# Attention pairs with q and k in 1.5 KB runs, evacuations ordered ahead of masks, and full-row stores

## The chip, the cores and the metric

The kernel runs on one core of a Trainium2 chip. The time is device microseconds (us) from launch to the end of the program on that core. Before the change the median of three runs is 192.61 us, with 190.53 and 195.77 as lowest and highest. The profile is of one further execution, whose span is 193.9 us.

A core has five engines that run their own instruction lists in order: TensorE (PE, with its weight loads as PEld), VectorE (DVE), ScalarE (ACT), GpSimd (POOL) and SyncE (SP). Sixteen DMA engines move data between HBM and the on-chip SBUF. TensorE writes to PSUM, from which VectorE and ScalarE read. Between engines there are semaphores, which the tile framework places from the order of the statements; within an engine the order of the statements is the order of execution.

## The reference

Two steps. First attention over 4 batches of 8 heads, 768 tokens, head size 64. "Retrieval" heads see all earlier tokens; the other heads see only the first 4 tokens and the last 64. Then a soft mixture of experts over the 3072 tokens of width 512, with 8 experts of 4 slots.

```python
scores = scale * q @ k.T                      # per head, 768 x 768
mask = causal if head is retrieval else causal & (first 4 columns | last 64 tokens)
a = exp(scores where mask); a = a / a.sum(-1)
x = (a @ v) with heads side by side           # (4*768, 512)

logits = x @ phi                              # (3072, 32)
d = exp(logits); d /= d.sum(over tokens)      # dispatch
slot_input = d.T @ x                          # (32, 512)
slot_out[e] = relu(slot_input[e] @ w1[e]) @ w2[e]     # 8 experts, 4 slots each
c = exp(logits); c /= c.sum(over slots)       # combine
out = c @ slot_out                            # (3072, 512) float32
```

## The kernel before

The 32 heads are worked through as 16 pairs (n = 0 to 15), four pairs to a batch. A pair's exponentials come in six chunks (c = 0 to 5), each of up to 1024 elements per partition for the two heads. Weights, q, k and v are loaded as float32 and cast to bf16 by GpSimd's DMAs. The parts that matter:

```python
raw  = tile_pool("raw", bufs=3);  qkT = tile_pool("qkT", bufs=2);  vfp, ptp, xp: bufs=2
scp = PSUM pool, bufs=2 (scores, logits, expert and output sums)
trp = PSUM pool, bufs=2 (everything transposed);  pvp = PSUM pool, bufs=2

def load_qk(n, which):                        # 8 tokens = 2 KB to a partition, 96 partitions
    t = raw.tile([96, 2, 512], BF16)
    nc.gpsimd.dma_start(t, src[b, h:h + 2].rearrange("h (p s) d -> p h (s d)", s=8))

def transposes(n, which):
    tp = trp.tile([P, 8, 96], BF16, tag="tr")
    ... 16 TensorE transposes of 96x64
    if which == "q":   # the queries end up in a permuted token order
        nc.vector.tensor_copy(dst.rearrange("c (i s p) -> c i s p", s=8, p=16),
                              tp.rearrange("c s (i p) -> c i s p", p=16))
    else:
        nc.vector.tensor_copy(dst.rearrange("c (p s) -> c p s", s=8), tp.rearrange("c s p -> c p s"))

def vfar(n):                                  # v times the head's far mask
    for i in range(2):
        nc.gpsimd.tensor_mul(t[:, i], vbs[n % 5][:, i, :4, :], fmask[...].to_broadcast([P, 4, 65]))

def scores(n, c):
    ... matmuls into sc
    nc.scalar.activation(pT[n][:, :, o:o + ln], sc[:, :, :ln], ACT.Exp, scale=scale)
    if c in (0, 1, 2): nc.vector.tensor_mul(x, x, m)      # near mask, at once

def pvmm(n, i): ...                           # rows i of a @ v, 65 columns (the last is the sum)
def norm(n, half): ...                        # reciprocal and multiply on VectorE, into xb
def x_transpose(n): ...                       # 6 transposes, one copy to xT on VectorE

def logits_exp(b):
    nc.scalar.activation(expC[b], lgs[b][:ES], ACT.Exp)                       # 32 x 768
    for c in range(2):                        # the same again, put back into token order
        nc.scalar.activation(expT[:, b, 384*c:384*(c+1)].rearrange("c (i p s) -> c i s p", s=8, p=16),
                             lgs[b][:, c, :384].rearrange("c (i s p) -> c i s p", s=8, p=16),
                             ACT.Exp, accum_out=colpart[...])

# set-up on VectorE: masks, then a column of ones in all five v buffers
transposes(0, "k"); transposes(0, "q"); head_mask(0); head_mask(1)
for t in vbs: V.memset(t[:, :, :, D:], 1.0)

for n in range(NP + 1):
    load_qk(n + 3, "k"); load_qk(n + 3, "q"); load_v(n + 3); w_load(1 or 2); vfar(n)
    for c in range(6):
        scores(n, c)
        # last = n - 1, the pair before
        c == 0: pvmm(last, 0..2); norm(last, 0)
        c == 1: transposes(n + 1, "q")
        c == 2: pvmm(last, 3); x_transpose(n - 2)
        c == 3: transposes(n + 1, "k");  if n % 4 == 1: logits_mm(b, all); logits_exp(b)
        c == 4: pvmm(last, 4);           if n % 4 == 2: dispatch(b)
        c == 5: pvmm(last, 5); norm(last, 1)
        # n % 4 == 2, c == 0: exp_tokens(b)
    n < 3: two more head_masks on VectorE

... last w2 loads, in halves of 256 columns
x_transpose(15); logits_mm(3, (3,)); logits_exp(3); exp_tokens(3); dispatch(3)   # whole batch at a time
... slot sums, 64 expert matmuls "hp", relu, 16 transposes, 24 small row sums "rp"

# second expert matmul and outputs, one half of 256 columns after the other
for e4, gs in ((0, (0, 1, 2, 3)), (1, (0, 1))):
    for x in range(2): second(x, e4, gs)
for x in range(2):
    for g in (2, 3): second(x, 1, (g,))
    V.tensor_copy(slot_out[:, cs], sp[x])
    for t in range(6):
        op = scp.tile([P, 4, 256], F32)       # 4 matmuls of 256 columns
        V.tensor_mul(ots[t][:, 0:2, cs], op[:, 0:2], rrow...)
        for r in (2, 3): nc.scalar.activation(ots[t][:, r, cs], op[:, r], ACT.Copy, scale=rrow...)
        nc.sync.dma_start(ov[:, 4*t:4*t+4, cs], ots[t][:, :, cs])    # runs of 1 KB
```

Of the kernel before, what the change touches and what calls it, by code (L numbers as in the profile page):

```python
# [38 lines left out]
def kernel(  # L39
# [41 lines left out]
    phif = single([P, 4, ES], F32, "phif")  # L81
# [10 lines left out]
    fmask = single([P, H, 4], BF16, "fmask")  # L92
# [5 lines left out]
    r1 = single([P, H], F32, "r1")  # L98
    thr = single([P, H], F32, "thr")
    vbs = [single([P, 2, 6, 65], BF16, f"vb{i}") for i in range(5)]  # L100
# [3 lines left out]
    def load_qk(n, which):  # L104
        b, h = n // 4, 2 * (n % 4)
        src, d = (q, qraw) if which == "q" else (k, kraw)
        t = raw.tile([96, 2, 512], BF16, tag="r" + which, name="r" + which)
        nc.gpsimd.dma_start(t, src[b, h:h + 2].rearrange("h (p s) d -> p h (s d)", s=8))  # L108
        d[n] = t
# [25 lines left out]
    def transposes(n, which):  # L135
        src = (qraw if which == "q" else kraw)[n]
        tp = trp.tile([P, 8, 96], BF16, tag="tr", name="tp" + which)
        for s in range(8):
            for hh in range(2):
                nc.tensor.transpose(tp[64 * hh:64 * hh + 64, s, :], src[:, hh, 64 * s:64 * s + 64],  # L140
                                    ident[:96, :96])
        dst = qkT.tile([P, S], BF16, tag="T" + which, name="T" + which)
        if which == "q":
            nc.vector.tensor_copy(dst.rearrange("c (i s p) -> c i s p", s=8, p=16),  # L144
                                  tp.rearrange("c s (i p) -> c i s p", p=16))
            qT[n] = dst
        else:
            nc.vector.tensor_copy(dst.rearrange("c (p s) -> c p s", s=8), tp.rearrange("c s p -> c p s"))  # L148
            kT[n] = dst

    def vfar(n):
        h = 2 * (n % 4)
        t = vfp.tile([P, 2, 4, 65], BF16, tag="vf", name="vf")
        for i in range(2):
            nc.gpsimd.tensor_mul(  # L155
                t[:, i], vbs[n % 5][:, i, :4, :],
                fmask[:, h + i, :].rearrange("p (j o) -> p j o", o=1).to_broadcast([P, 4, 65]))
        vf[n] = t

    def scores(n, c):  # L160
# [11 lines left out]
        nc.scalar.activation(pT[n][:, :, o:o + ln], sc[:, :, :ln], ACT.Exp, scale=scale)  # L172
        h = 2 * (n % 4)
        if c == 0:
            x, m = pT[n][:, :, 0:512], msk[:, h:h + 2, 0:512]
        elif c == 1:
            x = pT[n][:, :, 512:1024].rearrange("p h (a c) -> p h a c", a=2)
            m0 = msk[:, h:h + 2, 256:512]
            m = bass.AP(tensor=m0.tensor, offset=m0.offset, ap=[m0.ap[0], m0.ap[1], [0, 2], [1, 256]])
        elif c == 2:  # L180
            x, m = pT[n][:, :, 1024:1408], msk[:, h:h + 2, 256:640]
        else:
            return
        nc.vector.tensor_mul(x, x, m)  # L184

    def pvmm(n, i):
        if i % 3 == 0:
            pv[n] = pvp.tile([P, 3, 2, 65], F32, tag="pv", name="pv")
        for hh in range(2):
            for j in range(i + 1):  # L190
                vv = vbs[n % 5] if i - j <= 1 else vf[n]
                o = BLK[j, i]
                nc.tensor.matmul(pv[n][:, i % 3, hh, :], pT[n][:, hh, o:o + 128], vv[:, hh, j, :],  # L193
# [12 lines left out]
    def x_transpose(n):  # L206
        b, hp = n // 4, n % 4
        tp = trp.tile([P, S], BF16, tag="tr", name="tpx")
        for i in range(6):
            nc.tensor.transpose(tp[:, i * 128:(i + 1) * 128], xb[b][:, i, hp * 128:(hp + 1) * 128], ident)  # L210
        nc.vector.tensor_copy(xT[:, hp], tp)
# [3 lines left out]
    def logits_mm(b, dbs):  # L215
        if dbs[0] == 0:
            lgs[b] = scp.tile([P, 2, 512], F32, tag="sc", name="lg")
        for db in dbs:
            for c in range(2):
                nc.tensor.matmul(lgs[b][:, c, :384], phi4[:, db].rearrange("p g s -> p (g s)"), xT[:, db, 384 * c:384 * (c + 1)],  # L220
                                 start=(db == 0), stop=(db == 3))

    def logits_exp(b):
        expC[b] = small.tile([ES, S], BF16, tag="expC", name="expC")
        nc.scalar.activation(expC[b].rearrange("c (a t) -> c a t", a=2), lgs[b][:ES, :, :384], ACT.Exp)
        for c in range(2):
            nc.scalar.activation(  # L227
                expT[:, b, 384 * c:384 * (c + 1)].rearrange("c (i p s) -> c i s p", s=8, p=16),
                lgs[b][:, c, :384].rearrange("c (i s p) -> c i s p", s=8, p=16),
                ACT.Exp, accum_out=colpart[:, 2 * b + c:2 * b + c + 1])  # L230

    elgs = {}
    expC = {}

    def exp_tokens(b):
        tp = trp.tile([P, 6, ES], BF16, tag="tr", name="tpe")
        for i in range(6):
            nc.tensor.transpose(tp[:, i, :], expC[b][:, i * 128:(i + 1) * 128], ident[:ES, :ES])
        elgs[b] = small.tile([P, 6, ES], BF16, tag="elg", name="elg")
        nc.vector.tensor_copy(elgs[b], tp)  # L240

    def dispatch(b):
        sp = trp.tile([P, DM], F32, tag="tr", name="slp")
        for i in range(6):
            g = i % 4
            nc.tensor.matmul(sp[32 * g:32 * g + 32, :], elgs[b][:, i, :], xb[b][:, i, :],
                             start=(i < 4), stop=(i + 4 >= 6))
        if b == 0:
# [5 lines left out]
        else:  # L254
            nc.vector.tensor_copy(slot_bf[:, 1], sp)
# [6 lines left out]
    nc.sync.dma_start(phif, moe_phi.rearrange("(do di) s -> di do s", di=P))  # L262
    diff = single([P, P], F32, "diff")
    dist = single([P, 256], F32, "dist")
    nc.gpsimd.iota(diff, pattern=[[1, P]], base=0, channel_multiplier=-1,
                   allow_small_or_imprecise_dtypes=True)
    load_v(0)
    nc.gpsimd.iota(dist[:, :P], pattern=[[1, 8], [8, 16]], base=0, channel_multiplier=-1,
                   allow_small_or_imprecise_dtypes=True)
# [10 lines left out]
    V.tensor_single_scalar(ident, diff, 0.0, op=ALU.is_equal)  # L280
# [4 lines left out]
    V.tensor_scalar(dist[:, P:], dist[:, :P], float(P), None, op0=ALU.add)  # L285
    V.tensor_single_scalar(ge, dist, 0.0, op=ALU.is_ge)
    V.scalar_tensor_tensor(grade[:, 256:512], dist, float(window), ge, op0=ALU.is_lt, op1=ALU.mult)
# [8 lines left out]
    V.tensor_copy(fmask, r1.rearrange("p (h o) -> p h o", o=1).to_broadcast([P, H, 4]))  # L296
    V.tensor_scalar(fmask[:, :, 0], r1, sk, None, op0=ALU.max)
# [4 lines left out]
    transposes(0, "k")  # L302
    transposes(0, "q")
    for h in range(2):
        head_mask(h)
    for t in vbs:
# [13 lines left out]
    for n in range(NP + 1):  # L320
        live = n < NP
        if live:
            if n + 3 < NP:
                load_qk(n + 3, "k")
                load_qk(n + 3, "q")
                load_v(n + 3)
            w_load(2 if n % 3 == 2 else 1)
            vfar(n)
        if n == 0:
            nc.gpsimd.tensor_copy(phi4, phif.rearrange("p (a o) s -> p a o s", o=1).to_broadcast([P, 4, 4, ES]))  # L330
        for c in range(6):
            if live:
                scores(n, c)
            if n >= 1:
                if c == 0:
                    if n == NP:
                        x_transpose(n - 2)
                    for i in range(3):
                        pvmm(n - 1, i)
                    norm(n - 1, 0)  # L340
                    if n == NP:
                        logits_mm(B - 1, (0, 1, 2))
                elif c == 2:
                    pvmm(n - 1, 3)
                    if n >= 2 and live:
                        x_transpose(n - 2)
                elif c >= 4:
                    pvmm(n - 1, c)
                    if c == 5:
                        norm(n - 1, 1)  # L350
            if n + 1 < NP and c in (1, 3):
                transposes(n + 1, "q" if c == 1 else "k")
            b, r = n // 4 - 1, n % 4
            if b >= 0 and n < NP:
                if r == 1 and c == 3:
                    logits_mm(b, (0, 1, 2, 3))
                    logits_exp(b)
                elif r == 2 and c == 0:
                    exp_tokens(b)
                elif r == 2 and c == 4:  # L360
                    dispatch(b)
# [10 lines left out]
    for half in range(2):  # L372
        nc.gpsimd.dma_start(w2s[5][:, 4 * half:4 * half + 4], w2v[5][:, 4 * half:4 * half + 4])
    for e in (6, 7):
        w2s[e] = ptp.tile([P, 8, DM], BF16, tag="pT", name=f"w2_{e}")
    for c0 in (0, 256):
        for e in (6, 7):
            nc.gpsimd.dma_start(w2s[e][:, :, c0:c0 + 256], w2v[e][:, :, c0:c0 + 256])


    x_transpose(NP - 1)
    logits_mm(B - 1, (3,))
    logits_exp(B - 1)
    exp_tokens(B - 1)
    dispatch(B - 1)
# [45 lines left out]
    sp = [pvp.tile([P, 256], F32, tag="pv", name=f"sp{x}") for x in range(2)]  # L431

    def second(x, e4, gs):
        for fo in range(8):
            for g in gs:
                nc.tensor.matmul(sp[x][32 * g:32 * g + 32, :], hT[e4][:, fo, 32 * g:32 * g + 32],  # L436
                                 w2s[4 * e4 + g][:, fo, 256 * x:256 * x + 256],
                                 start=(e4 == 0 and fo == 0), stop=(e4 == 1 and fo == 7))

    ots = [single([P, 4, DM], F32, f"ot{t}", tag=f"w1_{t}") for t in range(6)]  # L440

    ov = out.rearrange("(p r) d -> p r d", r=24)

    def outputs(x):
        cs = slice(256 * x, 256 * x + 256)
# [54 lines left out]
```

## Time and profile before

| what | from the page |
|---|---|
| time, median of 3 | 192.61 us (190.53 to 195.77) |
| span of the profiled execution | 193.9 us |
| granted TensorE clock, mean | 0.855 |
| busy: PE, ACT, DVE, POOL | 130.1, 113.2, 111.4, 80.9 us |
| software DMA queue (all loads but two small ones) | 26.22 MB, 94.3% of the 16 engines' span |
| hardware DMA queue (the stores) | 6.37 MB, 10.0% |

A pair's first exponential on ScalarE marks its beginning in the timeline. From there the trace falls into: set-up and pair 0 (to 21.9 us), pairs 1 to 14 (21.9 to 139.5), pair 15 with the last batch's logits (139.5 to 155.0), the experts' first layer (155.0 to 164.05), and the second layer with the outputs (164.05 to the end). No engine is busy throughout: the busiest, PE, is at 67%, and part of its busy time is spent at a reduced clock. "Idle before, releaser" in the groups tells what ended an engine's waits; the chain of waits tells which of them set the end.

### The profile page before, as it was taken

What the parts mean: (1) busy time and instruction counts of PE and PEld (TensorE: products, weight loads), DVE (VectorE), ACT (ScalarE), POOL (GpSimd) and SP (SyncE); (2) the same over time, 40 slices, a digit from 0 to 9 for tenths busy, and PEclk for the clock granted to TensorE, in tenths of its full rate; (3) what the DMA queues carried; (4) which work ended last, traced back from release to release, by engine and by line L of the source; (5) the groups of instructions that cost most, each with busy time, mean ns of one, the idle gap of its engine ahead of it and who ended that gap; (6) DMA issues with size and microseconds to landing.
All of it is one profiled execution on the core that took longest, in us unless ns stands there. A gap on an engine that the chain in (4) does not pass through costs nothing.

```text
span 193.9 us, 4565 instructions
## 1 busy us (share of the span) xinstructions
PE 130.1 (67%) x1968; PEld 86.1 (44%) x1968; DVE 111.4 (57%) x227; ACT 113.2 (58%) x144; POOL 80.9 (42%) x119
## 2 busy tenths in 40 slices
PE   0380695984962996976299697729976498958420
PEld 0340363652641654654165465426553137845410
DVE  1912899699590689489067957807684313054620
ACT  2082495775649776775977686596780713036440
POOL 7931995746660645756064874103264000000000
PEclk9999997599699588799958879995899579696995
DMA  5999999999999789999949999954189999419997
GB/s 71 154 195 198 182 179 191 211 196 194 167 186 162 66 137 170 134 209 171 156 32 162 169 195 187 213 101 74 37 133 210 208 170 198 66 44 339 338 341 236
DMA packets 46707, 32.86 MB, mean 169 GB/s; under 512 B 26720, under 2 KB 43104, under 8 KB 46688
## 3 DMA queue, kind: packets, MB, share of 16 engines
q0 software_dynamic: 39680, 26.22, 94.3%
q1 hardware_dynamic: 7008, 6.37, 10.0%
q8 instruction: 15, 0.25, 0.5%
q14 instruction: 4, 0.03, 0.0%
HBM read 52.50 MB, written 6.29 MB: 303 GB/s over the span
## 4 chain that ended last, share of the span: by engine, by line
PE 43%; DVE 22%; ACT 17%; DMA 7%; issue 5%; POOL 2%; ACTq 0%; POOLq 0%; DVEq 0%
PE pv L193 11%; PE sc L167 10%; DVE pT L184 9%; ACT expT L227 7%; ACT pT L172 6%; PE tpk L140 4%; PE sp L436 4%; DVE xb L202 4%; DMA vb<-in_v_dram 4%; DMA rk<-in_k_dram 3%; PE lg L220 3%; PE hp L405 3%; PE op L450 3%; DVE Tq L144 2%; ACT ot L454 2%
## 5 line engine op out<-in xcount | busy, mean ns | idle before, releaser
L172 ACT ACTIVATE pT<-sc 128x1024 bf16<-128x1024 f32 (+1 forms) x96 | 84.4, 928 | 39.8 <-PE sc L167 36.9
L167 PE MATMUL sc<-Tq,Tk 64*128 64x256 bf16 (+3 forms) x320 | 41.8, 332 | 20.7 <-ACT expT L227 10.8
L184 DVE TENSOR_TENSOR pT<-pT,msk 128x1024 bf16<-128x1024 bf16 (+1 forms) x48 | 36.9, 773 | 10.0 <-ACT pT L172 9.7
L193 PEld LDWEIGHTS <-pT 128*128 128x128 bf16 x672 | 29.3, 109 | 14.5 <-issue 13.2
L193 PE MATMUL pv<-vb,pT 128*128 128x65 bf16 x352 | 31.5, 212 | 0.0
L155 POOL TENSOR_TENSOR vf<-vb,fmask 128x260 bf16<-128x260 bf16 x32 | 22.8, 732 | 18.0 <-PE pv L193 11.4
L193 PE MATMUL pv<-vf,pT 128*128 128x65 bf16 x320 | 28.5, 211 | 0.0
L114 POOL DMA_DIRECT2D vb<-in_v_dram x16 | 16.9, 1057 | 26.6 <-issue 20.1
L167 PEld LDWEIGHTS <-Tk 64*128 64x128 bf16 x320 | 12.5, 99 | 31.0 <-issue 15.2
L140 PE MATMUL tpk<-ident,rk 96*64 96x96 bf16 x256 | 10.6, 236 | 21.6 <-DVE Tq L144 14.5
L140 PEld LDWEIGHTS <-rk 96*64 96x64 bf16 x256 | 9.0, 129 | 25.5 <-issue 19.6
L201 DVE RECIPROCAL rs<-pv 128x6 f32<-128x6 f32 x32 | 6.1, 191 | 24.1 <-PE pv L193 24.1
L108 POOL DMA_DIRECT2D rk<-in_k_dram x16 | 11.1, 696 | 20.2 <-PE tpk L140 18.9
L202 DVE TENSOR_TENSOR xb<-pv,rs 128x384 bf16<-128x384 f32 x32 | 17.8, 558 | 1.1
L454 ACT ACTIVATE ot<-op,rrow 128x256 f32<-128x256 f32 x24 | 9.5, 473 | 14.2 <-DVE ot L451 14.2
L148 DVE COPY Tk<-tpk 128x768 bf16<-128x768 bf16 x16 | 15.2, 948 | 1.1 <-PE tpk L140 1.0
L227 ACT ACTIVATE expT<-lg 128x384 bf16<-128x384 f32 x8 | 14.2, 2014 | 0.0
L140 PE MATMUL tpq<-ident,rq 96*64 96x96 bf16 x256 | 10.8, 241 | 1.2 <-DMA rq<-in_q_dram 1.2
L450 PE MATMUL op<-slot_out,expT 128*128 128x256 bf16 x48 | 7.6, 296 | 5.7 <-ACT ot L454 4.3
L451 DVE TENSOR_TENSOR ot<-op,rrow 128x512 f32<-128x512 f32 x12 | 8.1, 690 | 5.7 <-PE op L450 5.6
L140 PEld LDWEIGHTS <-rq 96*64 96x64 bf16 x256 | 8.2, 133 | 5.8 <-issue 3.9
L108 POOL DMA_DIRECT2D rq<-in_q_dram x16 | 10.3, 645 | 0.5 <-issue 0.3
(69 smaller groups left out, 133.1 us busy)
## 6 DMA issues: line engine op xcount, KB each, us to landing
w<-in_moe_w_dram POOLq DMA_DIRECT2D x32, 512.0 KB, 8.7
out_dram<-ot SPq DMA_DIRECT2D x12, 512.0 KB, 4.2
rk<-in_k_dram POOLq DMA_DIRECT2D x16, 192.0 KB, 6.7
rq<-in_q_dram POOLq DMA_DIRECT2D x16, 192.0 KB, 7.0
vb<-in_v_dram POOLq DMA_DIRECT2D x16, 192.0 KB, 6.4
phif<-in_moe_phi_dram SPq DMA_DIRECT2D x1, 64.0 KB, 2.6
ri<-in_is_retrieval_dram SPq DMA_DIRECT2D x1, 8.0 KB, 2.6
```

Source lines behind the costliest of these rows:

```text
L108: nc.gpsimd.dma_start(t, src[b, h:h + 2].rearrange("h (p s) d -> p h (s d)", s=8))
L114: nc.gpsimd.dma_start(vbs[n % 5].rearrange("p h j d -> p (h j) d")[:, :, :D], a.rearrange("h (j p) d -> p (h j) d", p=P))
L140: nc.tensor.transpose(tp[64 * hh:64 * hh + 64, s, :], src[:, hh, 64 * s:64 * s + 64], ident[:96, :96])
L148: nc.vector.tensor_copy(dst.rearrange("c (p s) -> c p s", s=8), tp.rearrange("c s p -> c p s"))
L155: nc.gpsimd.tensor_mul(t[:, i], vbs[n % 5][:, i, :4, :], fmask[:, h + i, :].rearrange("p (j o) -> p j o", o=1).to_broadcast([P, 4, 65]))
L167: nc.tensor.matmul(sc[:, hh, at:at + 128 * cnt], kT[n][po:po + 64, j * 128:(j + 1) * 128], qT[n][po:po + 64, i0 * 128:(i0 + cnt) * 128], s ...
L172: nc.scalar.activation(pT[n][:, :, o:o + ln], sc[:, :, :ln], ACT.Exp, scale=scale)
L184: nc.vector.tensor_mul(x, x, m)
L193: nc.tensor.matmul(pv[n][:, i % 3, hh, :], pT[n][:, hh, o:o + 128], vv[:, hh, j, :], start=(j == 0), stop=(j == i))
L202: nc.vector.tensor_mul(xb[b][:, 3 * half:3 * half + 3, h * D:(h + 2) * D].rearrange("p i (h d) -> p i h d", h=2), pv[n][:, :, :, :64], rs. ...
L227: nc.scalar.activation(expT[:, b, 384 * c:384 * (c + 1)].rearrange("c (i p s) -> c i s p", s=8, p=16), lgs[b][:, c, :384].rearrange("c (i ...
L450: nc.tensor.matmul(op[:, r], er[4 * t + r], slot_out[:, cs], start=True, stop=True)
```

## The change

It is a bundle of rearrangements within the same algorithm.

* **q and k in natural order**: six tokens (1.5 KB) to a partition on 128 partitions in place of eight on 96. The token order inside a pair is now the natural one, so the permuted exponential of the logits becomes a plain one, and the separate 32-row exponential falls away (its rows are read from the same result).
* **Evacuations**: q's transposes are copied out by VectorE ahead of the masks; k's go to ScalarE, after the fifth exponential. Both write contiguously from a strided PSUM pattern.
* **Far mask**: the multiply of v moves from GpSimd to VectorE, as one operation on full operands; the mask is expanded once by 16 ScalarE copies at the start.
* **Masks** are separate statements, one step behind their exponentials.
* **The last pair and batch in halves**, so that parts of the chain can overlap; the last slot sum and `slot_out` are split between ScalarE and VectorE.
* **Outputs in full rows**: the second expert matmul is 512 columns wide, outputs alternate between VectorE and ScalarE row by row, and the stores carry whole rows of 2 KB, in groups of 1, 1, 2 and then 4 rows; the late w2 loads carry whole rows as well.

```diff
-        t = raw.tile([96, 2, 512], BF16, tag="r" + which, name="r" + which)
-        nc.gpsimd.dma_start(t, src[b, h:h + 2].rearrange("h (p s) d -> p h (s d)", s=8))
+        t = raw.tile([P, 2, 384], BF16, tag="r" + which, name="r" + which)
+        nc.gpsimd.dma_start(t, src[b, h:h + 2].rearrange("h (p s) d -> p h (s d)", s=6))
...
+    def evac(n, which, tp):
+        o, i = dst.rearrange("c (p s) -> c p s", s=6), tp.rearrange("c s p -> c p s")
         if which == "q":
+            nc.vector.tensor_copy(o, i)
         else:
+            nc.scalar.copy(o, i)
...
-        for i in range(2):
-            nc.gpsimd.tensor_mul(t[:, i], vbs[n % 5][:, i, :4, :], fmask[...].to_broadcast([P, 4, 65]))
+        nc.vector.tensor_mul(t, vbs[n % 5][:, :, :4, :], fmask[:, h:h + 2])      # 128 x 528
...
-    def logits_exp(b):
-        nc.scalar.activation(expC[b]..., lgs[b][:ES, :, :384], ACT.Exp)
-        for c in range(2):
-            nc.scalar.activation(expT[...].rearrange("c (i p s) -> c i s p", s=8, p=16), ...)
+    def logits_exp(b, c):
+        nc.scalar.activation(expT[:, b, 384 * c:384 * (c + 1)], lgs[b][:, c, :384], ACT.Exp,
+                             accum_out=colpart[:, 2 * b + c:2 * b + c + 1])
...
-            nc.vector.tensor_copy(slot_bf[:, 1], sp)
+            nc.scalar.copy(slot_bf[:, 1, :256], sp[:, :256])
+            nc.vector.tensor_copy(slot_bf[:, 1, 256:], sp[:, 256:])
...
-    for t in vbs:
+    V.memset(vbs[0][:, :, :, D:], 1.0)
+    for h in range(H):
+        nc.scalar.copy(fmask[:, h], r1[:, h:h + 1]...to_broadcast([P, 4, 66]))
+        nc.scalar.copy(fmask[:, h, 0], r0[:, h:h + 1].to_broadcast([P, 66]))
+    for t in vbs[1:]:
         V.memset(t[:, :, :, D:], 1.0)
...
+    # order within pair n (last = n - 1)
+        scores(n, 0); pvmm(last, 0..2)
+        scores(n, 1); norm(last, 0); tq = transposes(n + 1, "q"); evac(n + 1, "q", tq); mask(n, 0)
+                      n % 4 == 2: exp_tokens(b)
+        scores(n, 2); pvmm(last, 3); x_transpose(n - 2); mask(n, 1)
+        scores(n, 3); tk = transposes(n + 1, "k"); n % 4 == 1: logits_mm(b, all); mask(n, 2)
+        scores(n, 4); evac(n + 1, "k", tk); pvmm(last, 4); vfar(n)
+                      n % 4 == 1: logits_exp(b, 0); logits_exp(b, 1)
+        scores(n, 5); pvmm(last, 5); norm(last, 1); n % 4 == 2: dispatch_mm(b); slot_sum(b)
...
+    # after the loop: pair 15's rows 0-2, norm, x_transpose(14), rows 3-5, norm, logits of 3 blocks,
+    # then x_transpose, logits, exponential, tokens and dispatch each in two halves of 384 tokens
...
-    (second matmul and outputs for 256 columns, then for the other 256)
+    for e4, gs in ((0, (0, 1, 2, 3)), (1, (0, 1)), (1, (2,)), (1, (3,))):
+        second(e4, gs)                          # 512 columns
+    V.tensor_copy(slot_out[:, :256], sp[:, :256])
+    nc.scalar.copy(slot_out[:, 256:], sp[:, 256:])
+    for t, rows in enumerate((1, 1, 2, 4, 4, 4, 4, 4)):
+        for y in range(0, rows, 2):
+            op = scp.tile([P, 2, DM], F32)
+            ... one 512-column matmul per row; odd rows scaled by ScalarE, even ones by VectorE
+        nc.sync.dma_start(ov[:, r - rows:r, :], ot)
```

## The prediction

> **What bounds the kernel now.** I read, in this order: the engine and clock rows of the page, the costliest groups with each shape apart, the waits, the chain of waits in a stretch around one logits batch, the timeline of ScalarE, and the landing times of the DMAs. The groups first:
>
> ```profile
> L172 ACT ACTIVATE pT<-sc 128x1024 bf16<-128x1024 f32 x64 | 65.3, 1040 | 38.1 <-PE sc L167 35.3 <-ACT pT L172 1.3 <-DVE xb L202 1.1
> L184 DVE TENSOR_TENSOR pT<-pT,msk 128x1024 bf16<-128x1024 bf16 x32 | 28.3, 887 | 10.0 <-ACT pT L172 9.7
> L148 DVE COPY Tk<-tpk 128x768 bf16<-128x768 bf16 x16 | 15.2, 948 | 1.1 <-PE tpk L140 1.0
> L227 ACT ACTIVATE expT<-lg 128x384 bf16<-128x384 f32 x8 | 14.2, 2014 | 0.0
> L144 DVE COPY Tq<-tpq 128x768 bf16<-128x768 bf16 x16 | 8.7, 547 | 0.0
> ```
>
> A permuted exponential of 384 elements takes 2014 ns, twice one of 1024. ScalarE's exponentials wait 35.3 us for scores, so ScalarE is starved, not saturated. What starves it stands in the chain from 86 to 99 us (start, length, what):
>
> ```profile
> 88.74 0.96 DVE pT L184
> 89.70 0.48 DVE Tq L144
> 90.18 0.04 issue
> 90.22 0.53 PE tpk L140 x16
> 90.75 1.42 PE lg L220 x8
> 92.17 0.02 issue
> 92.20 0.80 ACT expC L225
> 93.00 3.46 ACT expT L227 x4
> 96.45 0.04 issue
> 96.50 0.34 PE sc L167 x2
> ```
>
> The reader is to see two things. A mask on VectorE stands ahead of q's evacuation; k's transposes need a PSUM buffer that this evacuation frees; and the next scores stand behind those transposes on in-order TensorE. The waits put 14.5 us on "PE tpk <- DVE Tq". Second, once a batch the three logits exponentials (4.26 us) hold up everything.
>
> The timeline's first exponentials of the pairs give the pace. Pairs 2, 3, 4, 7, 8, 11 and 12 take 8.32, 6.84, 8.80, 7.93, 6.51, 7.51 and 6.80 us (52.7). The logits pairs 5, 9 and 13 take 12.41, 11.99 and 11.38 (35.8). The dispatch pairs 6, 10 and 14, which follow them, take 7.64, 7.63 and 7.96 (23.2). Sum: 111.7 us from 27.80 to 139.52.
>
> **What the skill says.** (1) The Trainium skill, "ScalarE: Activation LUTs", What ACT_TABLE_LOAD costs: an ACTIVATE with immediate scale takes 186 ns plus 0.833 ns an element, and neighbours overlap by about 93 ns. The trace agrees: 1039 ns worked out and 1040 measured for 1024 elements. A plain 384-element one would be 506 ns. (2) "SBUF — State Buffer", Specifications: 16-byte cachelines, with a penalty when an access goes to a new line. The permuted expT writes at a step of 16 bytes and pays 2014 in place of 506, so the trace fits. (3) "VectorE: DVE Perf Modes", The perf-mode tier table: a PSUM source allows at most the 2x mode; the section on what the auto-detection checks ties it to unit step. Tq with unit runs takes 547 ns, Tk with strided reads 948, so q's new evacuation should cost 948. (4) "GPSIMD Engine Reference", Specifications: its SBUF interfaces are shared with VectorE, with contention for two-input operations. Masks take 0.69 us in undisturbed stretches and 1.15 at 82.13 us beside GpSimd's multiply; this too fits.
>
> **The change, part by part.**
>
> Start. VectorE's column of ones in the third v buffer still stands behind that buffer's load (landed 18.00 us). After it come q's evacuation (0.95), so pair 1 can start at about 19.8 us, against 21.9. The 16 new ScalarE copies, about 5 us as an estimate (0.41 and 0.24 us, 186 ns + 0.833 an element), delay pair 0's exponentials from 10.1 to about 13 us, but its masks wait for 18 us anyway. But rows of pair 0 need masks (0.69 + 0.69 + 0.55), the far multiply and then the pair's head masks on VectorE, which hold pair 1 back by about as much. I put pair 2 at 27.7 us, against 27.80: gain 0.1.
>
> Ordinary pairs. ScalarE: six exponentials back to back take 4.96 us in pair 15 (139.52 to 144.48). k's evacuation adds 768 elements, 186 + 640 = 826 ns. Sum 5.79, with hand-overs 6.05. In the order of the code, k's evacuation follows the fifth exponential; the next pair's first scores (0.45 us to the first exponential) run beside the sixth, 0.59 us, so there is hardly a gap. VectorE: masks 0.69 + 0.69 + 0.55, q 0.95, far multiply about 0.41 (between the mask's 768 elements at 545 and 1024 at 690, continued to 528), norms 1.50, xT 0.55: 5.34 us, against 5.86 before. TensorE: 4.75 us busy in pair 8 at clock 1.00; transposes keep their columns (12 x 128 for 16 x 96). So ScalarE is the tightest at 6.05. With the head masks of the first pairs and stretches of low clock I take 6.5: 7 x 6.5 = 45.5, against 52.7.
>
> Logits pairs. The permuted pair with expC, 0.80 + 3.46, becomes two plain ones with their accumulator reads, 2 x (0.5 + 0.5) = 2.0 us. But TensorE's eight logits matmuls (1.42 us) still stand between k's transposes and chunk 4, db 3 waiting for VectorE's xT, and hold ScalarE for about 1.5 us; the two exponentials take 2.0; the sixth chunk's scores wait for the logits' PSUM buffer, 0.5 and then 0.4. So 6.05 + 4.5 = 10.6: three make 31.8, against 35.8.
>
> Dispatch pairs. TensorE idles some 3 us ahead of them, and the clock follows it down: in pair 14 the granted clock is 0.62 and PE is busy for 7.96 of 7.96 us. I keep most of it: 7.4, three 22.2, against 23.2.
>
> Pairs 2 to 14: 45.5 + 31.8 + 22.2 = 99.5, against 111.7: **gain 12.2 us**.
>
> The last batch. Before: from pair 15's last exponential (144.48) to the first expert matmul (155.03) 10.55 us. After, counted from the same point: rows 0-2 at 1.3, norm 2.3, rows 3-5 3.1, three logits blocks 4.15, first half transposed, copied and multiplied 5.2, its exponential 6.35, the second's 7.4; then tokens, copy and dispatch 8.5. The slot sum's halves come after one another, not side by side: in the timeline the two readers of one PSUM tile (ACT hs 158.46 to 159.15, DVE hs from 159.18) take turns. So 0.4 + 0.45, then sums and siT: 10.2. Gain 0.3. The halves save the exponential's wait and lose it in more hand-overs.
>
> First layer to second: 155.03 to 164.05, unchanged.
>
> Outputs. Before, the first store is issued 8.92 us after the second layer begins (172.97), and the landings end at 192.88, one every 1.54 us for 0.52 MB, 340 GB/s, without a hole. This is a **DMA-bound** end. After: the second layer takes its whole 8.3 us first (6.19 + 2.12 today), slot_out in two turns 1.1, one matmul 0.35, one row 0.75: first store at 10.5. Larger packets help a little: from the landings, k's 192 packets of 2 KB take about 1.07 us and v's 1536 of 256 B about 1.37; on 16 engines that is 89 and 14.3 ns, or 3.6 ns and 0.0417 ns a byte. Full rows would thus run at up to 384 GB/s: 6.29 MB in 16.4 us. Production (0.69 + 0.69 + 0.62 us for two operations of two rows in turn, 1.03 us a pair of rows, 12.4 in all) is faster than that. End: 10.5 + 1.43 (2.98 to the first landing less 1.55) + 16.4 = 28.3, against 28.83. Gain 0.5.
>
> Sum: 0.1 + 12.2 + 0.3 + 0.5 = 13.1 us; 192.6 - 13.1 = **179.5 us**.
>
> **The rivals.** (a) *ScalarE's evacuation of k is slow.* VectorE copies the strided PSUM pattern in 948 ns without a further penalty, but no ScalarE operation of the trace reads such a pattern; if it lost as the permuted expT does, 768 elements at some 3 ns more each would be about 2.5 us or more, and 14 pairs would lose 20 us and more: 195 to 205 us. For it: expT's 2014 ns. Against: expT's stride is on the SBUF write, here the write is contiguous. I give it one chance in ten. (b) *TensorE becomes the bound.* At clock 0.62 a pair costs 7.96 us. Should the clock stay low, ordinary pairs stop at 7.3 and the gain is about 6: 187 us. Against: pair 8 ran at 1.00, and the stalls that bring the clock down get shorter. If instead it stays high, dispatch pairs fall to 6.6 too: 176. (c) *Loads become the bound.* A pair's k, q, v take 3.5 us of DMA time and 1.33 weights of 2.2 us each 2.9, together 6.4 of the new 6.5. For it: the software queue's 94.3% of the span. Against: loads are issued over two pairs ahead, GpSimd no longer holds them behind its multiply, and logits pairs give 4 us to catch up. If the lead is used up: 183. (d) *Stores gain nothing from long rows*: 340 GB/s again, 2 us later: 181.5.
>
> **Range and chances.** (b), (c) and (d) move the result by 2 to 8 us, and the runs before lie 5 us apart: 172 to 188. Faster by over 2% means under 188.8: 0.87. Within 2% 0.09, slower 0.04, nearly all of it rival (a).
>
> **What would show it.** k's copy on ScalarE at 0.8 to 0.9 us (2 us or more: rival a). No waits of PE tpk for DVE Tq; masks at 0.69. expT at about 1 us with its read. Logits pairs at 10 to 11 us, with the wait of scores behind lg, ordinary ones at 6 to 6.6. Pair 2 still at 27 to 28 us. First store about 10.5 us after the second layer begins, and a full DMA row to the end. The prediction is wrong if ordinary pairs stay over 7.3, or if the last batch or the outputs move by more than 3 us.

## The result and the profile after

The median falls from 192.61 to **169.66 us** (three runs, 168.63 to 170.73): ratio 0.886, 95% interval 0.868 to 0.903. The prediction was 179.5 us, with a range of 172 to 188. The direction was right, the size was not: 22.9 us gained against 13.1 foreseen, and the result lies 2.3 us below the range.

The groups of the profile after, each shape apart, for the lines shown of before. Columns: line, engine, operation, operands, count, then busy us and mean ns, then idle time before and what ended it.

```profile
L171 ACT ACTIVATE pT<-sc 128x1024 bf16<-128x1024 f32 x64 | 63.1, 1029 | 7.6 <-PE sc L166 7.0
L183 DVE TENSOR_TENSOR pT<-pT,msk 128x1024 bf16<-128x1024 bf16 x32 | 21.7, 682 | 0.2 <-ACT pT L171 0.2
L147 DVE COPY Tq<-tpq 128x768 bf16<-128x768 bf16 x16 | 15.3, 957 | 5.5 <-PE tpq L140 5.5
L150 ACT COPY Tk<-tpk 128x768 bf16<-128x768 bf16 x16 | 13.0, 814 | 3.8 <-PE tpk L140 3.8
L171 ACT ACTIVATE pT<-sc 128x768 bf16<-128x768 f32 x16 | 13.0, 815 | 1.6 <-PE sc L166 1.6
L223 ACT ACTIVATE expT<-lg 128x384 bf16<-128x384 f32 x8 | 3.9, 502 | 3.9 <-PE lg L219 3.9
L223 ACT ACTIVATION_READ_ACCUMULATOR expT<-lg 128x1 f32 x8 | 1.7, 212 | 0.0
```

The durations came as worked out: masks 682 ns, q's copy 957, k's copy on ScalarE 814 (826 as an estimate from the Trainium skill, "ScalarE: Activation LUTs", What ACT_TABLE_LOAD costs), the plain exponential 502 (506, an estimate from the same section). k's copy takes what an exponential of 768 elements in natural order takes, 815 ns, so rival (a), a slow strided read on ScalarE, is out. ScalarE now waits 7.0 us for scores in this shape, where it waited 35.3.

The timeline of ScalarE around ordinary pairs shows how close it runs (start, length, what):

```profile
87.27 1.05 ACT L171 ACTIVATE pT<-sc 128x1024 bf16<-128x1024 f32 x1
88.17 0.84 ACT L150 COPY Tk<-tpk 128x768 bf16<-128x768 bf16 x1
88.85 5.18 ACT L171 ACTIVATE pT<-sc 128x512 bf16<-128x512 f32 x6
93.87 0.84 ACT L150 COPY Tk<-tpk 128x768 bf16<-128x768 bf16 x1
```

From copy to copy 5.70 us, no gap, the six exponentials between them in one piece. In pairs 2 to 14 the granted TensorE clock averages 0.96 (0.83 before). But the chain that ended last no longer runs through the pairs:

```profile
DMA 36%; PE 8%; DVE 8%; issue 3%; POOL 1%; ACT 1%; POOLq 0%
```

Of it, 29% are the DMAs of the weights. The queue of loads runs without a hole until the last weights land at 139.11 us, and the second layer waits 1.44 us for them (engine and what it waited for; us in total, times, longest):

```profile
PE sp L470 <- DMA w<-in_moe_w_dram: 1.4, 1, 1.4
```

By the prediction's own pieces, from first exponentials, the first matmuls of each layer, and landings (before, the timeline has the second layer's first matmul at 163.98 us, 0.07 ahead of the border used so far):

| piece, us | before | foreseen | after |
|---|---|---|---|
| pair 2 starts | 27.80 | 27.7 | 24.57 |
| ordinary pairs 2, 3, 4, 7, 8, 11, 12 | 52.7 | 45.5 | 40.3 |
| logits pairs 5, 9, 13 | 35.8 | 31.8 | 24.8 |
| dispatch pairs 6, 10, 14 | 23.2 | 22.2 | 20.5 |
| pair 15's last exponential to the first layer | 10.55 | 10.2 | 8.2 |
| first layer | 8.95 | 9.05 | 9.6 |
| second layer to last landing | 28.9 | 28.3 | 34.6 |

Five pieces came out shorter than foreseen. The first layer (at a clock of 0.78, against 0.83 before) and the outputs came out longer, and hid part of the rest; the outputs are slower than before.

### The profile page after: what moved, and what is told of

Same layout as the page of the kernel before. It is cut to its first block, busy times and chain, and to the rows that moved or that the text cites. A ratio compares the mean times of both kernels' runs of the same rounds, so it can differ in the third digit from the quotient of the medians.

```text
span 168.9 us, 4098 instructions
## 1 busy us (share of the span) xinstructions
PE 121.2 (72%) x1751; PEld 72.0 (43%) x1752; DVE 102.0 (60%) x226; ACT 113.7 (67%) x162; POOL 58.6 (35%) x89
## 4 chain that ended last, share of the span: by engine, by line
DMA 36%; PE 8%; DVE 8%; issue 3%; POOL 1%; ACT 1%; POOLq 0%
DMA w<-in_moe_w_dram 29%; DMA rk<-in_k_dram 7%; PE op L486 7%; DVE ot L490 5%; DVE pT L183 1%; PE sp L470 1%; DVE Tq L147 1%; POOL vb L114 0%; ACT ot L488 0%; DVE xb L201 0%; POOL w L127 0%; POOL w L391 0%; PE pv L192 0%; DVE xT L210 0%; DVE slot_out L476 0%
## 5 line engine op out<-in xcount | busy, mean ns | idle before, releaser
L183 DVE TENSOR_TENSOR pT<-pT,msk 128x1024 bf16<-128x1024 bf16 (+1 forms) x48 | 29.3, 639 | 0.2 <-ACT pT L171 0.2
L192 PE MATMUL pv<-vb,pT 128*128 128x65 bf16 x352 | 27.7, 198 | 0.0
L486 PE MATMUL op<-slot_out,expT 128*128 128x512 bf16 x23 | 11.7, 599 | 11.0 <-DVE ot L490 10.1
L147 DVE COPY Tq<-tpq 128x768 bf16<-128x768 bf16 x16 | 15.3, 957 | 5.5 <-PE tpq L140 5.5
L488 ACT ACTIVATE ot<-op,rrow 128x512 f32<-128x512 f32 x12 | 8.3, 688 | 14.4 <-PE op L486 14.4
L490 DVE TENSOR_SCALAR ot<-op,rrow 128x512 f32<-128x512 f32 x12 | 9.0, 751 | 12.7 <-PE op L486 12.7
L150 ACT COPY Tk<-tpk 128x768 bf16<-128x768 bf16 x16 | 13.0, 814 | 3.8 <-PE tpk L140 3.8
L140 PE MATMUL tpk<-ident,rk 128*64 128x128 bf16 x192 | 9.4, 240 | 5.5 <-DMA rk<-in_k_dram 4.9
L140 PE MATMUL tpq<-ident,rq 128*64 128x128 bf16 x192 | 10.0, 251 | 3.0 <-DMA rq<-in_q_dram 3.0
L127 POOL DMA_DIRECT2D w<-in_moe_w_dram x16 | 9.0, 561 | 8.1 <-DMA w<-in_moe_w_dram 7.2
L140 PEld LDWEIGHTS <-rk 128*64 128x64 bf16 x192 | 6.7, 120 | 9.5 <-DMA rk<-in_k_dram 4.9
```

Of the source, the lines that this page charges most:

```text
L147: nc.vector.tensor_copy(o, i)
L150: nc.scalar.copy(o, i)
L486: nc.tensor.matmul(op[:, x], er[r], slot_out, start=True, stop=True)
L490: V.tensor_scalar(ot[:, y + x], op[:, x], rrow[:, r:r + 1], None, op0=ALU.mult)
```

## The experiments

e1, e2, e3 and e8 ran on one chip, e4 to e7 on a second, e9 to e12 on a third. The kernel before took 193.56, 191.99 and 192.71 us there, so differences of 1 to 2% between times from different chips say little. Ratios are to the kernel before on the same chip, with 95% intervals, without executions at a lowered clock; for e1 to e8 only four or five such executions of the kernel before were left and the verdict stayed unclear, though every interval ends below 0.98.

| run | time, us | ratio |
|---|---|---|
| e11, the changed kernel again | 169.60 | 0.880 (0.876 to 0.884) |
| e1, matmuls of a pair of rows first | 163.57 | 0.842 (0.835 to 0.850) |
| e8, old second layer and outputs | 164.65 | 0.849 (0.842 to 0.856) |
| e7, a PSUM tile for each row | 161.38 | 0.847 (0.839 to 0.855) |
| e3, logits in the old step | 180.94 | 0.934 (0.928 to 0.940) |
| e4, masks ahead of q's evacuation | 184.90 | 0.969 (0.962 to 0.977) |
| e5, k's evacuation on VectorE | 170.15 | 0.891 (0.881 to 0.900) |
| e6, far multiply on GpSimd | 169.25 | 0.889 (0.880 to 0.898) |
| e9, last batch in one piece | 169.28 | 0.878 (0.874 to 0.883) |
| e12, v buffers of 65 columns | 171.11 | 0.887 (0.883 to 0.892) |
| e10, e7 without the last weights | 159.20 | 0.826 (0.822 to 0.831) |
| e2, kernel before with 66 columns | 185.94 | 0.960 (0.953 to 0.968) |

e11 is the changed kernel without an edit:

> The changed kernel as it is, on the same chip as its neighbours: 169 to 171 us, ratio to the kernel before 0.88 to 0.89.

It came to that, and the others are held against it.

### The outputs: e1, e8, e7

In the changed kernel a pair of rows takes 1.855 us. The timeline of the output stage:

```profile
145.67 1.01 PE L486 MATMUL op<-slot_out,expT 128*128 128x512 bf16 x2 [0.84 <-DVE ot L490]
...
146.29 0.69 ACT L488 ACTIVATE ot<-op,rrow 128x512 f32<-128x512 f32 x1 [1.17 <-PE op L486]
146.72 0.75 DVE L490 TENSOR_SCALAR ot<-op,rrow 128x512 f32<-128x512 f32 x1 [1.10 <-PE op L486]
147.52 1.01 PE L486 MATMUL op<-slot_out,expT 128*128 128x512 bf16 x2 [0.84 <-DVE ot L490]
```

TensorE waits 0.84 us for VectorE, then VectorE 1.10 for TensorE. The statements read: matmul of row 0, scaling of row 0 (VectorE), matmul of row 1 into the other half of the same PSUM tile, scaling of row 1 (ScalarE). e1 only puts both matmuls first:

```diff
             for x in range(min(2, rows)):
-                nc.tensor.matmul(op[:, x], er[r], slot_out, start=True, stop=True)
+                nc.tensor.matmul(op[:, x], er[r + x], slot_out, start=True, stop=True)
+            for x in range(min(2, rows)):
                 if r % 2:
```

> The changed kernel with one edit: in the outputs both matmuls of a pair of rows stand ahead of the two scalings. Theory: in the changed kernel the odd row's matmul waits for VectorE's read of the even row in the same PSUM tile, because of the order of the statements, and with it the pair takes 1.855 us in place of about 1.03. Then a pair falls to 1.0 to 1.3 us and the time by 5 to 8 us, to 162 to 165 us. Rival: the outputs are slow because TensorE runs at a clock of 0.50 there; then the pair stays at 1.7 us or more and the time at 168 to 170 us.

Measured 163.57 us, and two pairs of rows in 2.57 us, 1.29 each. The clock stays at 0.50 in this stage, so the rival falls: order alone was worth some 6 us. What is left of the taking of turns shows here:

```profile
142.42 1.60 DVE L491 TENSOR_SCALAR ot<-op,rrow 128x512 f32<-128x512 f32 x2 [1.10 <-PE op L486]
...
143.20 0.69 ACT L489 ACTIVATE ot<-op,rrow 128x512 f32<-128x512 f32 x1 [1.53 <-DVE ot L491]
143.94 1.87 PE L486 MATMUL op<-slot_out,expT 128*128 128x512 bf16 x4 [0.71 <-ACT ot L489]
```

ScalarE's row, in the other half of the tile, still waits for VectorE's (1.53, DVE ot). e8 puts the old second layer and outputs, two halves of 256 columns, into the changed kernel:

```diff
-    sp = pvp.tile([P, DM], F32, tag="pv", name="sp")
-    ... (full rows)
+    sp = [pvp.tile([P, 256], F32, tag="pv", name=f"sp{x}") for x in range(2)]
+    ... (the kernel before, from here to the end)
```

> The changed kernel with the old second layer and outputs (two halves of 256 columns, stores in runs of 1 KB). Theory: the full-row outputs made this stage longer, 34.6 us from the second layer's first matmul to the last landing against 28.8 before; with the old stage it takes 28.5 to 30 and the time falls by 4.5 to 6 us, to 163.5 to 165 us. Rival: the stage is longer because the weights land late (a wait of 1.4 us) and the clock is low; then the old outputs stay at 32 us or more and the time at 167 us or more.

164.65 us; from the second layer's first matmul (131.49) to the last landing (161.81) 30.3 us, just over what was expected and clear of the rival. So the new stage costs 4 to 5 us against the old one (34.6 and 30.3 us; 169.60 and 164.65 in the whole). e7 gives each row a PSUM tile of its own:

```diff
-        for y in range(0, rows, 2):
-            op = scp.tile([P, 2, DM], F32, tag="sc", name="op")
-            for x in range(min(2, rows)): ...
+        for y in range(rows):
+            pool, tag = ((trp, "tr"), (pvp, "pv"))[r % 2]
+            op = pool.tile([P, DM], F32, tag=tag, name="op")
+            nc.tensor.matmul(op, er[r], slot_out, start=True, stop=True)
+            ... (even rows VectorE, odd rows ScalarE)
```

> The changed kernel with each output row in a PSUM tile of its own (four of one bank, two for VectorE's rows and two for ScalarE's). Theory: the turns of the two readers come from their sharing a PSUM tile, so with tiles of their own VectorE's 0.75 and ScalarE's 0.69 us run side by side, a pair of rows takes 0.8 to 1.05 us against 1.855 (1.29 where only the matmuls stood first), and the stores become the bound: 6.29 MB at 384 GB/s, as an estimate, 16.4 us and the last landing 26.5 to 27.5 us after the second layer begins; time 160.5 to 162.5 us. Rival: TensorE at a clock of 0.5, with 0.43 us for each matmul of 512 columns and its weights, or the stores hold it at 1.25 us a pair or more: time 163 us or more.

161.38 us, in the range of the theory. The timeline of e7:

```profile
140.94 8.72 PE L486 MATMUL op<-slot_out,expT 128*128 128x512 bf16 x24 [0.92 <-ACT slot_out L477]
...
141.57 8.77 DVE L490 TENSOR_SCALAR ot<-op,rrow 128x512 f32<-128x512 f32 x12 [1.08 <-PE op L486]
...
144.55 5.84 ACT L488 ACTIVATE ot<-op,rrow 128x512 f32<-128x512 f32 x9 [0.17 <-PE op L486]
```

All 24 rows are made in some 9 us, VectorE and ScalarE side by side, and the stores follow at one of 1 MB every 2.49 us, 421 GB/s. The granted clock rises in this stage of e7 (0.78 on average, against 0.50 in e1). But from 141.32 to 144.74 us, still at 0.50, e7's matmuls already follow one another every 0.43 us, 0.86 a pair of rows against 1.29 in e1, so the clock is not what made the difference. From first store to last landing: 19.9 us before, 25.2 in the changed kernel, 19.3 in e1, 20.0 in e8, 16.8 in e7. By this stage, full rows are worth about 3 us, once the engines keep up with them. The ratios do not show it: e1, e8 and e7 have 0.842, 0.849 and 0.847, with intervals that overlap. (Counted from the second layer's first matmul e7 takes 29.3 us, more than expected, since it began earlier and waited 2.8 us for weights.)

### The logits: e3

```diff
-        nc.scalar.activation(expT[:, b, 384 * c:384 * (c + 1)], lgs[b][:, c, :384], ACT.Exp,
+        nc.scalar.activation(expT[:, b, 384 * c:384 * (c + 1)].rearrange("c (i p s) -> c i s p", s=8, p=16),
+                             lgs[b][:, c, :384].rearrange("c (i s p) -> c i s p", s=8, p=16), ACT.Exp,
```

> The changed kernel, with the logits' exponentials written in the old step of 16 bytes (tokens within a block of 128 then stand in another order, so the output is not the reference's; the work is the same). Theory: the pace of the logits pairs (9.04, 7.92, 7.88 us) comes from the plain write: each pair of exponentials takes 3.4 us in place of 0.94, the accumulator's read 0.49 in place of 0.21, and pairs 5, 9 and 13 lengthen to 10.3 to 11.5 us. Time: four batches of 2.5 us less 1.4 us that the second layer waits for its last weights, 177 to 180 us. Rival: it is the missing 32-row exponential and the new place of the exponentials behind chunk 4 that made the pairs short; then they lengthen by under 1 us and the time is 169 to 172 us.

180.94 us, just over the range of the theory and far from the rival; logits pairs of 10.61, 10.39 and 10.61. The operations that touch expT in e3 (ns least, median, most):

```profile
L223 ACT ACTIVATE expT<-lg x8: 1866/1886/2199, 48.2 to 130.2; 128x384 bf16<-128x384 f32 x8
L223 ACT ACTIVATION_READ_ACCUMULATOR expT<-lg x8: 493/521/524, 49.6 to 131.6; 128x1 f32 x8
```

Against that, a logits pair of the changed kernel:

```profile
75.08 0.51 ACT L223 ACTIVATE expT<-lg 128x384 bf16<-128x384 f32 x1
75.46 0.21 ACT L223 ACTIVATION_READ_ACCUMULATOR expT<-lg 128x1 f32 x1
75.55 0.50 ACT L223 ACTIVATE expT<-lg 128x384 bf16<-128x384 f32 x1
75.92 0.22 ACT L223 ACTIVATION_READ_ACCUMULATOR expT<-lg 128x1 f32 x1
76.02 0.62 ACT L171 ACTIVATE pT<-sc 128x512 bf16<-128x512 f32 x1
```

The two take 0.94 us to the start of the next operation; the read lies mostly inside. The accumulator's read, 0.49 us in the kernel before, was long because the stepped write ahead of it was. The plain write is worth some 11 us, the largest single part after the order of the evacuations. That a step of 16 bytes costs this much fits the penalty for going to a new cacheline in the Trainium skill, "SBUF — State Buffer", Specifications; the page gives no size, the runs do: (1886 - 502) / 384 = 3.6 ns an element.

e3 also settles what shortened the last batch. From pair 15's last exponential to the first layer it takes 10.66 us (124.40 to 135.06), as before (10.55), although its last batch comes in halves as in the changed kernel (8.2). The first half's exponential, and then the second half's logits matmul behind it, first in e3, then that matmul in the changed kernel:

```profile
127.92 1.87 ACT L223 ACTIVATE expT<-lg 128x384 bf16<-128x384 f32 x1 [3.52 <-PE lg L219]
129.84 0.32 PE L219 MATMUL lg<-xT,phi 128*128 128x384 bf16 x1 [1.79 <-ACT expT L223]
```

```profile
119.39 0.32 PE L219 MATMUL lg<-xT,phi 128*128 128x384 bf16 x1 [0.50 <-ACT expT L223]
```

The matmul waits 1.79 us in place of 0.50, and the second exponential behind it is as long again.

### The order in the pair: e4, e5, e6

e4 puts two masks ahead of q's evacuation:

```diff
-            evac(n + 1, "q", tq)
         mask(n, 0)
+        mask(n, 1)
+        if n + 1 < NP:
+            evac(n + 1, "q", tq)
...
-        mask(n, 1)                      # after x_transpose
```

> The changed kernel with one edit: the first two masks of a pair stand ahead of q's evacuation on VectorE, as in the kernel before. Theory: q's evacuation then ends at about 4.4 us from the pair's first exponential in place of 3.3, k's transposes wait for it (PE tpk for DVE Tq comes back with 10 us or more in all), ScalarE gets a gap ahead of chunk 4, and an ordinary pair takes 6.5 to 7.5 us in place of 5.70; time 176 to 186 us. Rival: the pace comes from k's evacuation having left VectorE's list, and the order of the masks costs nothing; then ordinary pairs stay at 5.7 to 5.9 us and the time at 169 to 171 us.

184.90 us. Its timeline in pair 9:

```profile
79.16 0.69 DVE L183 TENSOR_TENSOR pT<-pT,msk 128x1024 bf16<-128x1024 bf16 x1 [0.16 <-ACT pT L171]
79.77 0.95 DVE L147 COPY Tq<-tpq 128x768 bf16<-128x768 bf16 x1
...
80.77 0.53 PE L140 MATMUL tpk<-ident,rk 128*64 128x128 bf16 x12 [1.14 <-DVE Tq L147]
...
83.07 1.02 ACT L171 ACTIVATE pT<-sc 128x1024 bf16<-128x1024 f32 x1 [2.32 <-PE sc L166]
```

The waits of e4 have it in all:

```profile
PE tpk L140 <- DVE Tq L147: 11.8, 10, 1.8
```

The chain shown of the kernel before is back: mask, q's copy, k's transposes waiting for it, scores, a gap on ScalarE. Ordinary pairs take 6.73 us in six of seven, and the logits and dispatch pairs lengthen as well (9.1 and 8.6 to 8.7). Order within VectorE's list alone is worth some 15 us (17 by the ratios).

e5 moves k's copy to VectorE:

```diff
-            nc.scalar.copy(o, i)
+            nc.vector.tensor_copy(o, i)
```

> The changed kernel with k's evacuation on VectorE in place of ScalarE, at the same place in the order. Theory: VectorE's list of a pair grows from 5.3 to 6.3 us and passes ScalarE's 5.70 less 0.81; ordinary pairs take 6.2 to 6.6 us, time 174 to 180 us. Rival: ScalarE sets the pace, and 0.81 us less on it make ordinary pairs 5.0 to 5.5 us; the time then falls little, since the last weights land at 139 us whatever the pace: 167 to 169.5 us.

Half of each came true. Ordinary pairs average 6.3 us (6.10, 6.52, 7.33, 6.39, 5.71, 6.39, 5.71), as the theory had it; but logits and dispatch pairs, where ScalarE is the tighter, shorten to 7.2 and 5.9 to 6.3. Pair 15 starts at 107.17 us, earlier than in e11 (109.34), yet the time is 170.15: the last weights land at 138.50 in e5 and 138.18 in e11. e6 moves the far multiply back:

```diff
-        nc.vector.tensor_mul(t, vbs[n % 5][:, :, :4, :], fmask[:, h:h + 2])
+        for i in range(2):
+            nc.gpsimd.tensor_mul(t[:, i], vbs[n % 5][:, i, :4, :], fmask[:, h + i])
...
         w_load(2 if n % 3 == 2 else 1)
+        vfar(n)                         # in place of after pvmm(last, 4)
```

> The changed kernel with the far multiply on GpSimd, in two operations at the head of the pair as in the kernel before. Theory: the masks beside it lengthen from 0.68 to 0.8 to 1.1 us and GpSimd holds loads back behind the multiply, but VectorE sheds 0.43 us and ScalarE sets the pace: ordinary pairs 5.7 to 6.0 us; the loads' queue gets holes and the last weights land 0 to 4 us later; time 169 to 174 us. Rival: the move of the far multiply is what freed VectorE and the loads; then pairs go over 6.3 us and the time to 177 us or more.

169.25 us, most ordinary pairs 5.70, the last weights at 138.36. Some masks grow (up to 1.75 us, median 0.68). Pair 15 starts at 112.16 us, 2.8 later than in e11: pair 5 takes 10.82 us in place of 8.38, with TensorE waiting 1.2 us for the far product. In the end nothing comes of it, as e11's second layer waits 1.43 us for its last weights and e6's does not. Neither engine move gains time in the whole, while the loads set the end.

### The start and the last batch: e2, e12, e9

```diff
-    vbs = [single([P, 2, 6, 65], BF16, f"vb{i}") for i in range(5)]
+    vbs = [single([P, 2, 6, 66], BF16, f"vb{i}") for i in range(5)]
```

(e2, in the kernel before; its matmuls and multiplies keep using 65 columns.)

> The kernel before with one edit: v buffers of 66 columns in place of 65 (the loads and the matmuls still use the same 65). Theory: with 65 columns the column of ones waits for the load of the same buffer, with 66 it does not, and this alone brings the start of the second pair's exponentials from 21.9 us to 16 to 19 us and pair 2 from 27.8 to 22 to 25 us, and the time from 192.6 to about 189 to 190 us. Rival: the early start of the changed kernel (17.6 us) comes from evacuations ahead of masks; then the wait of the memset stays at 7.9 us and pair 1 still starts at 21 to 22 us.

185.94 us, more than expected, from a pad. The columns of ones, first before, then e2 (last times: first and last start):

```profile
L307 DVE MEMSET vb<- x5: 68/68/68, 10.1 to 18.2; 128x12 bf16 x5
its engine sat idle before it (us, times) until:
  DMA vb<-in_v_dram: 7.9, 2
```

```profile
L307 DVE MEMSET vb<- x5: 78/78/78, 10.1 to 10.2; 128x24 bf16 x5
```

With 65 columns VectorE waits 7.9 us for loads into columns that it doesn't write; with 66 not at all. Pair 2 starts at 23.23 us, and GpSimd, which before held the fourth v load until the ones were set (6.5 us), runs ahead: by pair 5 e2 is at 43.21 us, against 51.76 before and 42.10 in the changed kernel. What in the width makes the framework see an overlap wasn't tried further. e12 undoes the pad in the changed kernel (v buffers, far mask and its product of 65 columns):

> The changed kernel with v buffers and far mask of 65 columns in place of 66. Theory: the columns of ones wait for their loads again, pair 1 starts at 20 to 21.5 us in place of 17.6 and pair 2 at 26.5 to 28 in place of 24.6, but most of it is taken up by the loads, whose queue ends 0.5 to 3 us later: 170 to 173 us. Rival: what the wider buffers gave the kernel before (7.6 us) they give here as well: 176 us or more.

171.11 us: pair 1 at 20.18, pair 2 at 28.39, pair 15 at 113.16, 3.8 us behind e11. Of that only 1.5 reach the time: the loads end at 140.19, and e12's second layer does not wait for its last weights, where e11's waits 1.43 us.

e9 puts the last batch together again:

```diff
-    x_transpose(last, 0, 3); logits_mm(bl, (3,), (0,)); logits_exp(bl, 0)
-    x_transpose(last, 3, 6); logits_mm(bl, (3,), (1,)); logits_exp(bl, 1)
-    exp_tokens(bl, 0, 3); dispatch_mm(bl, 0, 3); exp_tokens(bl, 3, 6); dispatch_mm(bl, 3, 6)
+    x_transpose(last); logits_mm(bl, (3,)); logits_exp(bl, 0); logits_exp(bl, 1)
+    exp_tokens(bl); dispatch_mm(bl)
...
-            nc.scalar.copy(slot_bf[:, 1, :256], sp[:, :256])
-            nc.vector.tensor_copy(slot_bf[:, 1, 256:], sp[:, 256:])
+            nc.vector.tensor_copy(slot_bf[:, 1], sp)
```

> The changed kernel with the last batch in one piece again: the last pair's transposes, logits, tokens and dispatch for all 768 tokens at a time, and one copy for the slot sum. Theory: the halves shorten the way from pair 15's last exponential to the first expert matmul, 8.2 us, which then grows to 9.5 to 10.6 us; but the last weights still land at about 139 us, so the time moves by under 1.2 us: 169.5 to 171 us. Rival (the prediction's reading, that the halves lose in hand-overs what they save): the way stays at 8 to 8.8 us.

The theory fell: the way takes 8.0 us in one piece (113.86 to 121.82), 8.2 in halves. The rival, the prediction's reading, holds. What shortened this way to 8.2 us is then not the halves but the plain write, as e3 shows; in the kernel before, the stepped exponentials' accumulators held back VectorE's sums until 154.15 us, 9.7 us after pair 15's last exponential.

### The wall behind it: e10

```diff
-    w2s[7] = ptp.tile([P, 8, DM], BF16, tag="pT", name="w2_7")
-    w2_late(7)
+    w2s[7] = w2s[6]
```

> The kernel with row tiles for the outputs, with the loads of the last expert's second weights (1 MB) left out; its matmuls read those of the expert before it, so the output is not the reference's. Theory: the loads are the wall behind the pairs, whatever their pace; the queue ends about 4.9 us earlier, at 133.2 us, and the time falls by 3.5 to 5 us, to 156.5 to 158 us. Rival: the second layer is held by TensorE's own path, and the wait for weights hides beside it; then the time falls by under 1.5 us, to 160 us or more.

159.20 us, between the two forecasts. The spans of e7 and e10, 160.4 and 156.9 us, differ by 3.5, the medians by 2.2, on different chips (ratios 0.847 and 0.826). e7's second layer waits 2.8 us for weights and e10's not at all, so a wait for weights it was, though less than all 4.9 us come out: the second layer now begins at 131.54 and runs without a wait, and TensorE's own path is next.

## Why the prediction was wrong, step by step

**Durations, the chain, the order: right.** That the pairs were held by masks ahead of q's evacuation and by the permuted exponentials stands (e4, e3), as do rival (a)'s rejection and the taking of turns of two readers of one tile (e7).

**Logits pairs, "So 6.05 + 4.5 = 10.6": failed, a mis-sized sum, 7.0 us in three.** Of the 4.5, the matmuls' hold was put at 1.5 and measured 1.1; "2 x (0.5 + 0.5) = 2.0 us" measured 0.94, the read taken over from the stepped write at 0.49 and added on top; the 0.9 us for PSUM hand-overs did not show. That 10.6 us is what e3 takes with the old step is chance.

**Ordinary pairs, "With the head masks of the first pairs and stretches of low clock I take 6.5": failed, 5.2 us in seven.** 0.26 us for hand-overs (5.79 to 6.05) and 0.45 for head masks and clock were allowances, not readings. The copy overlaps its neighbours as exponentials do, 4.96 + 0.81 less the overlap is 5.70, and the clock rose to 0.96. Dispatch pairs were 1.7 us too high in three; there the second half of rival (b) came true in part: the clock was 1.00, 0.78 and 0.76 in them, where before it was 0.67, 0.66 and 0.62, and they took 6.8 us on average (6.6 with the clock high).

**Start, "VectorE's column of ones in the third v buffer still stands behind that buffer's load": failed, 3.1 us.** I read 65 to 66 as alignment for the multiply and did not ask whether the wait was in the data. e2 shows that it was not.

**Last batch, "rows 0-2 at 1.3, norm 2.3": failed, 2.0 us too long.** These rows do not need the last exponential and were done at 115.0 us, 0.2 before it ended (115.24). Their norm, whose multiply is shown here, ended 0.9 us after it in place of 2.3:

```profile
115.61 0.56 DVE L201 TENSOR_TENSOR xb<-pv,rs 128x384 bf16<-128x384 f32 x1
```

That is 1.4 of the 2.0 us. That the halves bring nothing was right (e9), while the plain write brings 2.5 us here (e3: 10.66 against 8.2), where the whole gain was put at 0.3.

**Outputs, "Production (0.69 + 0.69 + 0.62 us for two operations of two rows in turn, 1.03 us a pair of rows, 12.4 in all) is faster than that": failed, 6.3 us the other way.** I had the two readers take turns, but read past the order of the statements, which makes the second matmul take its turn as well: 1.855 us a pair (e1, e7). So the engines, not the stores, set the end of this stage. The transfer rate was set too low, 384 GB/s against 421 in e7, but never mattered in the changed kernel; rival (d), that long rows gain nothing, is out by the 421.

**Rival (c), "Loads become the bound": right in another place.** Of pairs 2 to 14 only pair 5 is held by a load, and it takes 9.04 us where the other two logits pairs take 7.9:

```profile
43.91 0.53 PE L140 MATMUL tpq<-ident,rq 128*64 128x128 bf16 x12 [1.10 <-DMA rq<-in_q_dram]
```

But the queue ends at 138 to 140 us whether pair 15 starts at 107.2 (e5), 109.3 (e11) or 113.2 us (e12), and this is why e5, e6, e9 and e12 move so little.

The too-slow pieces sum to 19.0 us and the too-fast ones, outputs and first layer, to 6.9, which leaves 12 us; the spans, 193.9 and 168.9, gained 25.0 where 13.1 were foreseen. So the range was missed by sizes in the pairs, by a wait at the start that was not there and by an order in the last batch that was taken wrong, and the outputs hid a third of it.

The version to keep is e7: 161.38 us, ratio 0.847 (0.839 to 0.855), clear of the changed kernel's 0.880 (0.876 to 0.884). That it beats e1 (0.842) is seen in its output stage and not shown in the whole time.

## What to carry to other kernels

On in-order engines put first what frees a buffer for another engine, and last what nobody waits for: that order was worth some 15 us here, while two moves of work between engines were worth nothing once loads set the end. Before pricing a wait, ask whether the data need it: both a pad of one column and a swap of two statements took away waits that the data did not call for. And do not carry a companion's duration (the accumulator's read) over from a slow neighbour.

## What was not expected of the hardware

ScalarE reads a strided PSUM pattern at its full pace (768 elements in 814 ns), while a write to SBUF at a step of 16 bytes costs it 3.6 ns an element more and takes the accumulator's read from 0.21 to 0.52 us. Stores of four whole rows (8 KB in a run) ran at 421 GB/s in e7, those in runs of 1 KB at 340 in the kernel before. In pairs 2 to 14 the granted clock rose from 0.83 to 0.96, while TensorE was busy for 85% of the time (72.6 of 85.7 us) where it had been 75% (84.1 of 111.7); that the one brings the other is not shown.
